# A planned order of all engines, searched anew after the first TensorE operations get a higher price

## The chip, the cores and the metric

The kernel runs on one core of a Trainium2 chip. The core has five engines that work beside each other and wait for each other through semaphores: TensorE (PE in the profile; PEld is its loading of weights), VectorE (DVE), ScalarE (ACT), GpSimd (POOL) and SyncE (SP), which here only issues DMAs. The metric is the device time of one execution in microseconds (us).

## The reference

Cosine attention over 8 batches, 12 heads, 448 positions and 64 channels is followed by a layer of two matrix products with a gate between them:

```
q_n = q / (norm(q) + 1e-6);  k_n = k / (norm(k) + 1e-6)
attn = softmax(q_n @ k_n.T / tau);  a = attn @ v
x = a with heads side by side                # 3584 x 768
h = x @ w_in                                 # 768 x 2048
out = (h * sigmoid(1.702 * h)) @ w_out       # 2048 x 768
```

## The kernel before

**Tiles.** A "group" y is four heads of one batch; a batch has three groups, so that there are 24, y = 0 to 23. Two heads of a group form a pair x = 2y or 2y + 1. For a group, k and q are loaded by SP (L263 for group 0, L271 for the others), squared (`square`, L304 on VectorE or GpSimd, L305 on ScalarE), summed by VectorE (`reduce`, L313), turned into an inverse norm (batch 0: roots on ScalarE, L325, and reciprocals on VectorE, L336; later batches: Newton steps on VectorE, `norm_a` and `norm_b`, L344 to L372), and scaled (`scale`, L404 for k, L405 for q). Groups 0 to 4 are transposed by TensorE (`turn_qk`, L427, 7 transposes for k and 7 for q) and copied out of PSUM (L438); later groups are transposed by DMAs that SP issues (L445). The last keys are copied apart (`last_keys`, L454). TensorE makes scores into a PSUM tile "sp" with two buffers (L465, last keys L491), ScalarE makes exponentials of them (L500), and TensorE multiplies these with v (`attend`, L528 and L539, 14 matmuls for a pair and half of the positions); v is cast by `cast_v` (L416 to L421). VectorE normalises (L551, L567); the result x is transposed by TensorE (L577 for batch 0, L586) and copied (L604, L593), or by a DMA (L610).

**Two halves in batch 0.** In batch 0 (`first`) the scores are made for the first half of the query positions of all three groups (h = 0) and then for the second (h = 1), so that the products can begin with half of batch 0.

**Products.** `mm1_h` (L651, batch 0) and `mm1` (L621) multiply x with w_in. A unit is 12 matmuls of half width or 6 of full width; ScalarE takes its tanh (L631), VectorE multiplies ("gate", L663 or L638, result gT). A unit holds one of the four buffers of the PSUM tile "mm" until its gate is done; attention, transposes and the second products take the same four. `mm2` (L676) multiplies gT with w_out in parts of four matmuls; parts 0 and 1 of a product need the first half of w_out, parts 2 and 3 the second. `halve` (L689 on VectorE, L690 on ScalarE) scales the result into one of two output tiles, and two stores on SP (L695) free it.

**DMA queues.** Loads, stores and DMA transposes are issued by SP in the planned order, one behind the other; w_in (L700, eight pieces) and w_out (L706, two pieces) by GpSimd. The loads of groups 4 and 5 are held until pieces of w_in have landed, w_out until the load of q of group 5 has landed, and those of group 6 until all of w_out has landed (`HOLD`).

**What sets the order.** `Plan` (L61 to L183) has an entry for every operation: engine, duration in us, due time, operations it comes after, buffers that it takes and frees. `Plan.tune` shifts the due time of each operation by one letter of `DUES` (a quarter of a us for a step) and chooses for those with an alternative engine one by a digit of `ENGINES`. `Plan.order` then plays the durations through at building time and lets every engine take the ready operation with the least due time. The kernel's instructions are emitted in that order, and every engine carries out its own in order. Durations in the plan thus take no part in the run itself; they and the two strings, which a search found, set only who comes first and on which engine.

Of the kernel before, what the change touches and what calls it, by code (L numbers as in the profile page):

```python
# [29 lines left out]
    "L]Zj_ZKtWtgIZL]]dHKIFKJRtM6KKOSAL;R7DKKNKAKKKL4IQL?KKMKKNAMKOKITMtMKS#EKKPONKHBhIhEbK;XZkNKKQNUK/KEPKKEt"  # L30
    "KJAH5KKKKKKNYKgR#tL4D]dN=BNGIQtJhOKLHCK=Egs%E/UFUKJDQ4NK:KKBKKE^bPPGJtKTBEA+4FK^KD41BRK^NLGE_SVLEKSKFKPt"
    "IRJMKWGtUILRKI;Y/KJKKKKRC8KKKKKJKFNM@FCKMTKNKYSKJ(tKGLAFK9JKJHKJM:KHiVSKRBKK:CHnKV@l^KJNgLKKKLSKmqolSsqT"
    "_if>NtslUJ=tKtaKt^PtiQE5$SKtKistHDEIgKKnjpK2cdjat;A[KiDVt<LMD#KNb=ISKLMKT]t]GKaKAKKt_XK<Kko9s^XNJtLrb:Kt"
    "LKht]L8ttKGstCZEtKKcLKcMCKDKKF%KKTOGVme3DV?aSQGKIN?OOKOEM(JHdL/DVtIpKAOKEK]>KKQGjKKVtIKfKB>/U?RLGIKLWKKK"
    "tXA^KLGNNKKtkHKJjJVgt#DStKKsKbhKFA%,KsOKtpKKirKHKhtKsJtBrt2,XLKKcIMLJZJLgK_JKKCJKNSe@3E8UNDYWKK#UX#S^Nti"
    "KL9K_CtE:RTKNHOBKStIt5K.L^:%tJSKBKKtKKJ0#LKKpOOKKLKHKlgKDKLKKKVKDKTKKL3Q#hK#J#KKKHebHjKPV#KK3EW9@<#t#9WB"
    "RWII#TI#BKKJOMHK0JMH@LNZjWKK2CO;HM#BEM8X8pKKK#P/O(8K-KK%YH#WGGKX]QIK51Br<:F7IHY-(KKOTQcKHBKKZZ_aka^SLKK#"
    "..KM:A4KKTjBMGM<LFEQ5KI#LK<IIEWK@KK?&KK#I#KKYKmK#^+##;&*K4EGKKJ+Q3KQKHGFJ#JMT#)KUC#IG>XKKI@JDJKGHIIHK)OT"
    "SNKJKtKQUKgCcKY$UKsFYAKGTAKRZKKDVHKN4*E0%DfKI9TQPKNKCJK@>>KKKK%:%^6MKKAPH<;KNKH5KKN1KIkFKt4FD#BFMKKK<#KK"
    "<N<M^PEXK#VE5KKKKAI.KG#KJKDKUEK:LJUB#K<<KO&&bHNC#NKKK&FK6@0<K#S/Q%LKAL6K3)D,1/)P%U#9?#MK#KM#QM<OPCMM#MPZ"  # L40
    "t;2G#FB4=7KP5@7FKK1KK#K:-9=KtPKd;K8BNL_@D$KK:LKQEL>KKKFF+<KQDsFK0@3fIGGKKbG?KnDBL;KF9KKAKkfLKHMSQKPO[IPL"
    "R%KK)BjCnK$KKKL#PNJ_GSsFPCXM-NNLEJtKFDHK>mK#KKKL=_ZKeSJKBtj@NQHDfF&VKKNZIdEKKK0ITKDSSF#MKOH3RRKJ;O6K(6R^"
    "t)DK#KKFKPBOOEBDKCIKoLBKML==PKqSIKOM9JIs?K;IL@(LKKK=KHIGM9YPBWKOBVVKGKKXfLDKKTFDDDte@?EH-EKC##[YFKKOGK0N"
    "Q#M?[YKTHEQUR.K+@H#HKKF?K%PIK>INKG_UHQ>JV:CNDRVKRJNMIJKLHOKFI5-JFKDKKKGHMEUT>M_QONKK@#KYJTRRSJS($MDKHKIM"
    "KKK:DCF;=YK(KKNWZK^KKK[RRHFU;HP=KK;KL9$@OKKMQHQFE3MGB#MKF?,OHBW^##V=V56KPPWUETaMKSKHMK*IKBKLNBE@K@GJSKI#"
    "FtKttL"
)
ENGINES = (
    "00021100010101000101000001100010000001010200000011012001110101102001100120001000010001020100120000000210"
    "10021111001001000201101100111100000101200111020100100210000201001011100012011010121101021111101100000011"  # L50
    "0011110110001011000010101110101011101010100010"
# [135 lines left out]
def kernel(  # L187
# [535 lines left out]

    def due_of(y):
        return 2 * y if y < ND else 4 * y
# [12 lines left out]
    for y in range(NDUO):  # L738
# [53 lines left out]
        if y < TURNED:  # L792
            for ti in (1, 0):
                add(("tp", ti, y), "PE", 0.45, s - 3, partial(turn_qk, y, ti),
                    after=[("scale", ti, y)] + [("tp", 1, y)] * (not ti and y > 1), takes=[("mm", 1), ("qkT", ti)], frees=[("qks", 2)])
                add(("qkT", ti, y), "DVE", 0.65, s - 3, partial(turned_qk, y, ti), after=[("tp", ti, y)], frees=[("mm", 1)], alts=[("ACT", 0.92)])
# [11 lines left out]
        if first:  # L808
            for h in range(2):
                sh = s + 2 * ND * h  # L810
                behind = [("s", min(y + 1, ND - 1), 2, 0)] * h
                for g in range(3):
                    add(("s", y, g, h), "PE", 0.23, sh + 0.4 * g, partial(scores_h, y, g, h), after=ready + behind + [("s", y, 0, h)] * (g > 0),
                        takes=[("sp", 1), ("exp", int(h + g == 0))], rows=64)
                    add(("exp", y, g, h), "ACT", 0.92, sh + 0.4 * g + 0.1, partial(exp_h, y, g, h), after=[("s", y, g, h)], frees=[("sp", 1)])
                add(("s", y, "l", h), "PE", 0.19, sh + 0.6, partial(scores_l, y, h), after=ready_l + behind + [("s", y, 0, h)],
# [181 lines left out]
```

## Time and profile before

| | us |
|---|---|
| median of 5 runs (lowest, highest) | 432.1 (430.6, 432.86) |
| profiled execution: time | 431.62 |
| profiled execution: span from first to last instruction | 429.8 |
| busy: TensorE | 408.1 (95%) |
| busy: VectorE | 292.8 (68%) |
| busy: ScalarE | 253.8 (59%) |
| busy: GpSimd | 122.2 (28%) |

A row of the profile's timeline has a start and a duration in us, the engine, the line of the kernel, the operation, "out<-in" and a count where like instructions are merged; in brackets stands the idle time before it and what ended it. "PEclk" and the clock of a stretch are the TensorE clock that was granted, of 10 or of 1. Matmuls overlap, so the step from one start to the next, not the duration of one, is what a matmul costs in a row of them.

### The profile page before, as it was taken

What the parts mean: (1) busy time and instruction counts of PE and PEld (TensorE: products, weight loads), DVE (VectorE), ACT (ScalarE), POOL (GpSimd) and SP (SyncE); (2) the same over time, 40 slices, a digit from 0 to 9 for tenths busy, and PEclk for the clock granted to TensorE, in tenths of its full rate; (3) what the DMA queues carried; (4) which work ended last, traced back from release to release, by engine and by line L of the source; (5) the groups of instructions that cost most, each with busy time, mean ns of one, the idle gap of its engine ahead of it and who ended that gap; (6) DMA issues with size and microseconds to landing.
All of it is one profiled execution on the core that took longest, in us unless ns stands there. A gap on an engine that the chain in (4) does not pass through costs nothing.

```text
span 429.8 us, 9183 instructions
## 1 busy us (share of the span) xinstructions
PE 408.1 (95%) x3600; PEld 242.6 (56%) x3600; DVE 292.8 (68%) x710; ACT 253.8 (59%) x374; POOL 122.2 (28%) x200
## 2 busy tenths in 40 slices
PE   1789999889999999999999999999999999999996
PEld 0567887454556554655556555565556655655563
DVE  4797996669899868997889778659757315424500
ACT  5689875846656677766861578756665455204310
POOL 5666532272520713042432052462000000000000
PEclk9969999999999999999999999999999999999999
DMA  8999899997879994979969956969535340221022
GB/s 273 234 207 259 153 210 223 290 204 182 191 151 218 186 231 113 197 150 210 217 117 235 169 163 121 200 170 138 82 45 85 78 96 0 23 73 38 0 75 73
DMA packets 86538, 65.34 MB, mean 152 GB/s; under 512 B 54624, under 2 KB 81504, under 8 KB 86496
## 3 DMA queue, kind: packets, MB, share of 16 engines
q1 hardware_dynamic: 82304, 57.82, 62.4%
q0 software_dynamic: 3744, 6.29, 8.3%
q10 hardware_dynamic: 448, 0.66, 0.4%
q8 instruction: 28, 0.46, 0.4%
q14 instruction: 14, 0.11, 0.1%
HBM read 47.19 MB, written 11.01 MB: 135 GB/s over the span
## 4 chain that ended last, share of the span: by engine, by line
PE 86%; DMA 7%; ACT 3%; DVE 3%; SPq 0%; POOL 0%; issue 0%; ACTq 0%; POOLq 0%; DVEq 0%
PE mm L676 32%; PE mm L621 28%; PE mm L539 8%; PE sp L465 8%; DMA qk<-in_k_dram 4%; PE mm L651 4%; PE mm L528 3%; DMA qk<-in_q_dram 3%; PE sp L491 2%; ACT exp L500 2%; PE mm L427 1%; DVE qks L404 1%; DVE gT L638 1%; ACT sq L305 0%; POOL sq L304 0%
## 5 line engine op out<-in xcount | busy, mean ns | idle before, releaser
L500 ACT ACTIVATE exp<-sp 128x896 f16<-128x896 f32 (+1 forms) x171 | 147.2, 903 | 61.9 <-PE sp L465 53.4
L676 PE MATMUL mm<-w_out,gT 128*128 128x384 f16 x896 | 156.8, 326 | 0.0
L621 PE MATMUL mm<-xT,w_in 128*128 128x448 f16 x672 | 134.4, 353 | 2.0 <-ACT ost L690 1.4
L676 PEld LDWEIGHTS <-gT 128*128 128x128 f16 x896 | 83.8, 98 | 62.1 <-issue 9.6
L631 ACT ACTIVATE th<-mm 128x448 f16<-128x448 f32 x128 | 69.8, 547 | 56.6 <-PE mm L621 50.3
L621 PEld LDWEIGHTS <-w_in 128*128 128x128 f16 x672 | 64.0, 98 | 64.2 <-issue 7.0
L638 DVE SCALAR_TENSOR_TENSOR gT<-th,mm 128x448 f16<-128x448 f16 x112 | 67.9, 617 | 41.1 <-ACT th L631 39.7
L313 DVE TENSOR_REDUCE n<-sq 128x14 f32<-128x896 f32 (+1 forms) x50 | 51.7, 1043 | 10.2 <-ACT sq L305 6.8
L539 PE MATMUL mm<-vt,exp 128*128 128x65 f16 (+1 forms) x1152 | 57.4, 197 | 0.0
L539 PEld LDWEIGHTS <-exp 128*128 128x128 f16 (+1 forms) x1152 | 53.1, 101 | 2.3
L528 PE MATMUL mm<-vt,exp 128*128 128x130 f16 x192 | 43.5, 226 | 1.8 <-DVE xs L567 1.8
L465 PE MATMUL sp<-qkT 64*128 64x448 f16 (+1 forms) x324 | 42.9, 346 | 1.5 <-ACT exp L500 1.3
L567 DVE TENSOR_TENSOR xs<-mm,rc 112x256 f16<-112x256 f32 x96 | 40.7, 424 | 3.5 <-PE mm L577 0.2
L304 POOL TENSOR_TENSOR sq<-qk 128x896 f32<-128x896 f32 (+1 forms) x17 | 29.0, 1703 | 33.4 <-DMA qk<-in_q_dram 13.4
L689 DVE TENSOR_SCALAR ost<-mm 128x384 f32<-128x384 f32 x27 | 14.8, 554 | 34.7 <-PE mm L676 34.6
L454 POOL COPY kL<-qkT 64x128 f16<-64x128 f16 x36 | 13.2, 368 | 81.3 <-DVE vt L421 37.2
L690 ACT ACTIVATE ost<-mm 128x384 f32<-128x384 f32 x29 | 14.1, 494 | 35.8 <-PE mm L676 33.6
L551 DVE RECIPROCAL rc<-mm 112x4 f32<-112x4 f32 x96 | 17.0, 177 | 24.7 <-PE mm L539 23.9
L305 ACT ACTIVATE sq<-qk 128x896 f32<-128x896 f32 (+1 forms) x27 | 24.4, 907 | 13.6 <-DMA qk<-in_k_dram 5.8
L404 POOL TENSOR_TENSOR qks<-qk,y 128x384 f16<-128x384 f32 (+1 forms) x27 | 18.7, 721 | 39.5 <-DVE y L372 17.4
L416 POOL CAST vt<-v 128x384 f16<-128x384 f32 x28 | 15.6, 556 | 43.6 <-PE mm L539 18.9
L528 PEld LDWEIGHTS <-exp 128*128 128x128 f16 x192 | 19.4, 101 | 13.4 <-issue 8.1
(59 smaller groups left out, 266.1 us busy)
## 6 DMA issues: line engine op xcount, KB each, us to landing
v<-in_v_dram SPq DMA_DIRECT2D x48, 256.0 KB, 5.7
out_dram<-ost SPq DMA_DIRECT2D x54, 192.0 KB, 3.3
qk<-in_k_dram SPq DMA_DIRECT2D x23, 448.0 KB, 5.0
qk<-in_q_dram SPq DMA_DIRECT2D x23, 448.0 KB, 5.1
w_in<-in_moe_w_in_dram POOLq DMA_DIRECT2D x8, 384.0 KB, 14.8
w_out<-in_moe_w_out_dram POOLq DMA_DIRECT2D x2, 1536.0 KB, 15.2
qkT<-qks SPq DMA_TRANSPOSE x38, 4.5
xT<-xs SPq DMA_TRANSPOSE x18, 3.9
```

Of the source, the lines that this page charges most:

```text
L304: return engines[eng].tensor_tensor(out=dst, in0=src, in1=src, op=ALU.mult)
L305: return nc.scalar.activation(out=dst, in_=src, func=AF.Square)
L313: return nc.vector.tensor_reduce(out=n2s[y][:, ti, js], in_=sqs[y, ti][:, js], axis=AX.X, op=ALU.add,)
L465: nc.tensor.matmul(out=sp[:, j, at : at + qn], lhsT=qkT[r, g, 1, 128 * n : 128 * (n + 1)], rhs=qkT[r, g, 0, q0 : q0 + qn], start=True, sto ...
L500: return nc.scalar.activation(out=dst, in_=src, func=AF.Exp, scale=inv_tau, **ekw)
L528: nc.tensor.matmul(out=o, lhsT=e[:, (C - 1) * S + a : (C - 1) * S + a + m], rhs=vt[:, 3].rearrange("p j d -> p (j d)"), start=True, stop=F ...
L539: nc.tensor.matmul(out=o[:, (D + 1) * j : (D + 1) * (j + 1)], lhsT=e[:, at : at + m], rhs=vt[:, n, j], start=False, stop=n == 2, skip_grou ...
L567: return nc.vector.tensor_tensor(out=xs, in0=ps[:, :, :D], in1=r[:, :, None].to_broadcast((P, 4, D)), op=ALU.mult,)
L621: nc.tensor.matmul(out=ps[:, :S], lhsT=w_in_sb[:, kk, 128 * m : 128 * (m + 1)], rhs=xTs[b, kk], start=(kk == 0), stop=(kk == KT1 - 1),)
L631: nc.scalar.activation(out=ths[key], in_=mms[key][:, :S], func=AF.Tanh, scale=0.851)
L638: nc.vector.scalar_tensor_tensor(out=gts[b // 2][:, m, (b % 2) * S : (b % 2 + 1) * S], in0=ths.pop((b, m)), scalar=1.0, in1=mms.pop((b, m) ...
L676: nc.tensor.matmul(out=mms[b2, t, n][:, :NW], lhsT=gts[b2][:, kk, 128 * t : 128 * (t + 1)], rhs=w_out_sb[:, kk, NW * n : NW * (n + 1)], st ...
```

## The change

TensorE's operations of groups 0 and 1 in the first half (h = 0) have about double their old durations in the plan: 7 transposes 0.78 for 0.45 (groups 0 and 1, and k of group 2), scores 0.38 for 0.23, scores of last keys 0.36 for 0.19, attention of a pair 0.95 for 0.5, transposes of x 0.24 for 0.15. With these, the search was made anew: most letters of `DUES` and many digits of `ENGINES` are others. Lines behind L722 move down by three; those named above keep their numbers.

```diff
--- before.py
+++ after.py
@@ -27,28 +27,28 @@
 MOE_FROM, MOE_LAG = 8, 9
 STEPS = "#$%&()*+,-./0123456789:;<=>?@ABCDEFGHIJKLMNOPQRSTUVWXYZ[]^_abcdefghijklmnopqrst"
 DUES = (
-    "L]Zj_ZKtWtgIZL]]dHKIFKJRtM6KKOSAL;R7DKKNKAKKKL4IQL?KKMKKNAMKOKITMtMKS#EKKPONKHBhIhEbK;XZkNKKQNUK/KEPKKEt"
...
+    "QOKKQJKNLtKK#brJGVRLHLVELKOHFKKKKdKKHCRAP>RJLKVDLMKX&SK<KEWUK_HHJCWAJKHsFK:lKtKiUeP9O5KLC;NaOJJMKF4CqQMN"
...
 )
 ENGINES = (
-    "00021100010101000101000001100010000001010200000011012001110101102001100120001000010001020100120000000210"
...
+    "00021100111111100110101001100011001011101211000000010001110111120000011112011010000001200100020110002211"
...
 )
 
 
@@ -720,6 +720,9 @@
     for y in range(2 * ND, NDUO, ND):
         groups += [(y,), (y + 1, y + 2)]
     group_of = {y: g for g in groups for y in g}
+
+    def cold(y, h):
+        return y < 2 and not h
 
     def due_of(y):
         return 2 * y if y < ND else 4 * y
@@ -791,7 +794,7 @@
                 takes=[("vt", 1)], frees=[("v", g)], alts=[("DVE", 0.86)])
         if y < TURNED:
             for ti in (1, 0):
-                add(("tp", ti, y), "PE", 0.45, s - 3, partial(turn_qk, y, ti),
+                add(("tp", ti, y), "PE", 0.78 if first and y < 2 + ti else 0.45, s - 3, partial(turn_qk, y, ti),
                     after=[("scale", ti, y)] + [("tp", 1, y)] * (not ti and y > 1), takes=[("mm", 1), ("qkT", ti)], frees=[("qks", 2)])
                 add(("qkT", ti, y), "DVE", 0.65, s - 3, partial(turned_qk, y, ti), after=[("tp", ti, y)], frees=[("mm", 1)], alts=[("ACT", 0.92)])
             add(("kL", y), "POOL", 0.63, s - 2, partial(last_keys, y), after=[("qkT", 1, y)] + kept(y),
@@ -810,10 +813,10 @@
                 sh = s + 2 * ND * h
                 behind = [("s", min(y + 1, ND - 1), 2, 0)] * h
                 for g in range(3):
-                    add(("s", y, g, h), "PE", 0.23, sh + 0.4 * g, partial(scores_h, y, g, h), after=ready + behind + [("s", y, 0, h)] * (g > 0),
+                    add(("s", y, g, h), "PE", 0.38 if cold(y, h) else 0.23, sh + 0.4 * g, partial(scores_h, y, g, h), after=ready + behind + [("s", y, 0, h)] * (g > 0),
                         takes=[("sp", 1), ("exp", int(h + g == 0))], rows=64)
                     add(("exp", y, g, h), "ACT", 0.92, sh + 0.4 * g + 0.1, partial(exp_h, y, g, h), after=[("s", y, g, h)], frees=[("sp", 1)])
-                add(("s", y, "l", h), "PE", 0.19, sh + 0.6, partial(scores_l, y, h), after=ready_l + behind + [("s", y, 0, h)],
+                add(("s", y, "l", h), "PE", 0.36 if cold(y, h) else 0.19, sh + 0.6, partial(scores_l, y, h), after=ready_l + behind + [("s", y, 0, h)],
                     takes=[("sp", 1)], frees=[("qkT", h), ("kL", h)])
                 add(("exp", y, "l", h), "ACT", 0.55, sh + 0.7, partial(exp_l, y, h), after=[("s", y, "l", h)], frees=[("sp", 1)])
         else:
@@ -836,7 +839,7 @@
                 else:
                     at = s + 2 * g + 2 + 0.5 * h
                     es = [("exp", y, g, n) for n in range(3)] + [("exp", y, "l")]
-                add(("at", x, h), "PE", 0.5, at, partial(attend, x, h, first and not h), after=es + [("cast", x)] + [("at", x, 0)] * h + [("at", x - 1, 1)] * (g * h),
+                add(("at", x, h), "PE", 0.95 if first and cold(y, h) else 0.5, at, partial(attend, x, h, first and not h), after=es + [("cast", x)] + [("at", x, 0)] * h + [("at", x - 1, 1)] * (g * h),
                     takes=[("mm", 1)], frees=[("exp", g * h), ("vt", h)])
                 turned = y < TX
                 whole = turned and not first
@@ -844,7 +847,7 @@
                     after=[("at", x, h)] + [("nx", 2 * y, 0)] * (not turned and g + h > 0) + [("nx", x, 0)] * (whole and h),
                     takes=[("xs", int(turned if first else h == 0 and (turned or g == 0)))], frees=[("mm", int(not turned or (whole and h == 0)))])
                 if turned and first:
-                    add(("turn", x, h), "PE", 0.15, at, partial(turn_h, x, h), after=[("nx", x, h)], frees=[("xs", 1)])
+                    add(("turn", x, h), "PE", 0.24 if cold(y, h) else 0.15, at, partial(turn_h, x, h), after=[("nx", x, h)], frees=[("xs", 1)])
                     add(("x", x, h), "DVE" if h else "ACT", 0.28 if h else 0.35, at, partial(turned_h, x, h), after=[("turn", x, h)] + [("x", 2 * y, 0)] * (g + h > 0),
                         takes=[("x", 2 * (g + h == 0))], frees=[("mm", 1)],
                         alts=[("ACT", 0.35) if h else ("DVE", 0.28)])
```

The order in which each engine's instructions stand is fixed when the program is built, and so can be read for the new kernel too. What differs, in numbers:

| operation | before | after |
|---|---|---|
| squares of a whole q or k on ScalarE, GpSimd, VectorE | 24, 16, 6 | 21, 19, 6 |
| k scalings on VectorE, GpSimd | 14, 10 | 11, 13 |
| q scalings on VectorE, GpSimd | 12, 12 | 10, 14 |
| copies of transposed q or k on VectorE, ScalarE | 7, 3 | 5, 5 |
| casts of v (pairs) on VectorE, GpSimd | 20, 28 | 17, 31 |
| last-key copies on VectorE, GpSimd | 12, 36 | 24, 24 |
| half copies of x on VectorE, ScalarE | 10, 2 | 5, 7 |
| whole copies of x on VectorE, ScalarE | 2, 4 | 1, 5 |
| halvings on VectorE, ScalarE | 27, 29 | 23, 33 |
| TensorE before the first product with w_in: transposes of q and k, half scores, full scores, attention matmuls, x transposes | 56, 68, 4, 154, 20 | 56, 72, 0, 140, 18 |
| TensorE before the first part that needs the second half of w_out: half scores, full scores, attention matmuls, x transposes, mm2 | 68, 28, 280, 36, 8 | 72, 24, 238, 28, 8 |
| TensorE before the third unit of batch 1: half scores, full scores, mm2 | 68, 40, 92 | 72, 36, 96 |

In the order after, GpSimd scales q of group 1 before it issues w_in, and q of group 2 behind it; VectorE sums the squares of q of group 4 before the first gate (before: behind the second); ScalarE has the square of q of group 9 ahead of the first tanh of batch 1 (before: behind the second); SP has the loads of group 8 ahead of the first store, and the DMA transposes of group 6 ahead of the second.

## The prediction

> **What bounds the kernel now.** I read the page first (busy shares, the forty slices, the chain that ended last), then the stretches of two microseconds in the first 34, then TensorE's instructions in order of time, and last the landings and waits of the DMAs that TensorE needs.
>
> ```profile
> span 429.8 us, 9183 instructions
> PE 408.1 (95%) x3600; PEld 242.6 (56%) x3600; DVE 292.8 (68%) x710; ACT 253.8 (59%) x374; POOL 122.2 (28%) x200
> ...
> PEclk9969999999999999999999999999999999999999
> ...
> PE 86%; DMA 7%; ACT 3%; DVE 3%; SPq 0%; POOL 0%; issue 0%; ACTq 0%; POOLq 0%; DVEq 0%
> ```
>
> TensorE is busy 408.1 of 429.8 us and holds 86% of the chain: there are 21.7 us without a matmul. Its 3600 matmuls are the same after the change, so the time is TensorE's work plus its idle time plus the excess at a low clock. By TensorE's timeline the idle time is 7.97 before the first matmul, about 5 up to 30, 0.28 at 43, 1.84 at 84, 1.36 at 93, 0.68 at 104 and 4.1 behind the last matmul (0.49 for the last halving and the store). From 104.4 to 425.7 no gap shows.
>
> ```profile
> core 0: us, PE busy (x) PEld busy (x) DVE busy (x) ACT busy (x) POOL busy (x), PEclk, DMA share, GB/s
> 24.00:26.00 2.00, 1.97 (x15) 1.27 (x15) 1.95 (x5) 1.82 (x3) 1.79 (x5) 0.56 1.12 239
> 26.00:28.00 2.00, 1.56 (x16) 0.88 (x16) 1.96 (x5) 1.97 (x4) 1.60 (x3) 0.50 1.14 219
> 28.00:30.00 2.00, 2.00 (x26) 1.58 (x25) 1.46 (x6) 1.40 (x2) 0.92 (x3) 0.50 1.12 210
> 30.00:32.00 2.00, 2.00 (x32) 1.66 (x30) 1.73 (x8) 1.12 (x4) 0.00 (x0) 0.73 1.12 209
> ...
> 16.33 0.93 PE L427 MATMUL mm<-ident,qks 128*128 128x128 f16 x7
> ...
> 39.54 2.46 PE L651 MATMUL mm<-xT,w_in 128*128 128x224 f16 x24
> 43.48 2.46 PE L651 MATMUL mm<-xT,w_in 128*128 128x224 f16 x24 [0.28 <-DVE gT L663]
> ...
> 50.37 0.55 PE L427 MATMUL mm<-ident,qks 128*128 128x128 f16 x7
> ```
>
> In the stretches the tenth number, after five pairs of busy time and count, is the granted clock: 0.50 to 0.73 from 24 to 32. The seven transposes at 16.33 took 0.93 together, the same seven at 50.37 took 0.55, although the clock row has 1.00 at 16: matmuls ran slowly there too. So the old price of one transposing group (0.45) was too low early. The first product with w_in starts at 39.54.
>
> ```profile
> 67.64 1.46 PE L676 MATMUL mm<-w_out,gT 128*128 128x384 f16 x8
> ...
> 70.15 2.11 PE L676 MATMUL mm<-w_out,gT 128*128 128x384 f16 x12
> ...
> 85.91 0.23 PE L528 MATMUL mm<-vt,exp 128*128 128x130 f16 x1 [1.84 <-DVE xs L567]
> ...
> 94.36 2.43 PE L621 MATMUL mm<-xT,w_in 128*128 128x448 f16 x12 [1.36 <-ACT ost L690]
> ...
> 104.38 1.29 PE L621 MATMUL mm<-xT,w_in 128*128 128x448 f16 x6 [0.68 <-DVE gT L638]
> ```
>
> The products with w_out start at 67.64; the part that needs the second half of w_out is in the twelve at 70.15 (about 70.3, behind the last part of x = 8). Then come three stalls, 1.84 + 1.36 + 0.68 = 3.9.
>
> ```profile
> L706 POOL DMA_DIRECT2D w_out<-in_moe_w_out_dram x2: 893/920/946, 50.0 to 50.9; - x2
> DMA to landing us min/median/max: 11.6/15.2/18.8
> ...
> SPq L271 <- DMA w_in<-in_moe_w_in_dram: 18.0, 2, 10.5
> SPq L271 <- DMA w_out<-in_moe_w_out_dram: 3.0, 1, 3.0
> ```
>
> w_out is issued in two pieces at 50.0 and 50.9; they land 11.6 and 18.8 later, at 61.6 and 69.7. Loads behind them on SP wait for w_in and w_out pieces, 18.0 and 3.0 us. DMAs were busy more than 1.0 in nearly every stretch from 10 to 48 and again from 54 to 70. These landings are a clock that TensorE's order cannot hurry.
>
> **The change part by part.** (1) Only the planner's prices and the two search strings change. No matmul comes or goes: 0 us of work. Scores and transposes of groups 0 and 1 are spread differently on TensorE.
>
> (2) Other engines, by the rows' means and the new counts. VectorE loses three k scalings (2 x 0.813 + 0.304 each), two q scalings (1.1), three casts (0.55 + 0.23 + 0.27), two transposed copies (0.62), one whole and five half x copies (0.39, 0.27) and four halvings (0.55), and gains twelve last-key copies (0.21): about -13.7 us. ScalarE gains two transposed copies (0.91), five half and one whole x copy (0.36, 0.53), four halvings (0.49) and loses three squares (0.95): +3.3. GpSimd gains three squares (1.75), three k and two q scalings (2.2, 1.74), three casts (1.15) and loses twelve last-key copies (0.37): +14.3. They are busy 68%, 59% and 28%, TensorE's work lies over them: 0 on the path in total. If this cover went, the price is where one of them stands in front of a matmul, below.
>
> (3) Up to the first product. The new order copies both transposed halves of group 0 on ScalarE and squares group 2 before the first exponential: that starts near 15.4 instead of 14.88 (qkT of q at 13.85 + 0.91, then 0.56 of scores). GpSimd scales q of group 1 (1.69) before it issues w_in, so w_in starts near 18.7 instead of 17.34; behind its eight issues (5.2) comes the scaling of q of group 2, done at 25.5, where VectorE had it at 24.1. ScalarE's list from there to the last x copy is 12.6 us (eight or nine exponentials of 0.82 back to back, short ones of 0.46, copies) on top of about 23.3: 35.9 without gaps; with the 13% idle that it had in 20 to 40 about 38. Ends: 35.9 and, with the slow clock as long as now, 40.5. I take 38.5: a gain of 1, less 0.9 of work not yet done.
>
> (4) The gain is not kept. VectorE's new order puts the sum of squares of q of group 4 ahead of the first gate; before, two gates went first (42.8). That load landed at 41.5:
>
> ```profile
> 41.54 1.68 POOL L304 TENSOR_TENSOR sq<-qk 128x896 f32<-128x896 f32 x1 [3.44 <-DMA qk<-in_q_dram]
> ```
>
> So the first gate ends at 41.54 + 1.68 + 1.07 + 0.61 + 0.1 = 45.0, and the fourth product unit, which takes its PSUM buffer, starts then. Queued behind it on TensorE are attention and the other units. Counted by the steps from one matmul to the next at full pace in the rows (12 half-width products 1.15, 14 attention matmuls 0.50, 4 full scores 0.48), TensorE has done 20.7 us of work at 45.0; before, it had done 21.9 (25.0 at 48.08). Price at that point: 1.2, plus what the load slips.
>
> (5) w_out. Its issue waits for the load of q of group 5 and, on GpSimd, for k of group 4 to be scaled: 45.0 + 0.9 (Newton) + 0.6 (gate) + 0.3 + 1.3 + 2.0 = 50.1, against 49.96. Landings 61.7 and 69.8. Slip of w_in: between 0 (DMAs saturated, same bytes) and 1.3 (the later start); I take 1.0, nearest to the later start, because loads 4 and 5 wait for w_in pieces. At the part that needs the second half, the new order has done 42 attention matmuls (0.036 each), 8 x transposes (0.06) and 4 full scores (0.12) less and 4 half scores (0.075) more than the old: 1.5 + 0.5 + 0.5 - 0.3 = 2.2. It stands at 69.8 where the old was at 70.3 with 2.2 more done: +1.8 (rounded up for the switch between row modes), with the slip +2.8.
>
> (6) From 74 to 105. The old stalls of 3.9 belong to waits that are reordered (-3.9 if all go). New ones: on ScalarE the squares of k and q of group 7 stand before an exponential; k landed at 82.4, so that it ends near 85.9 and TensorE's next scores wait 1.2. The square of q of group 9 stands before the first tanh of batch 1; before, it stood behind two of them:
>
> ```profile
> 95.08 0.95 ACT L305 ACTIVATE sq<-qk 128x896 f32<-128x896 f32 x1 [0.33 <-DMA qk<-in_q_dram]
> ```
>
> Its load was issued at 86.46 and waited for until 95.08. Issued at 85.1 (the load whose completion it waits for, v of group 7, was issued at 73.3 and took 11.8) it lands between 93.6 and 95.0, then 0.95 + 0.54 + 0.61 until the third unit of batch 1 gets its buffer: 95.8 to 97.2, some 1.0 behind TensorE. The second store of the first output tile is queued behind the two transposes of group 6 on SP (5.4); the third tile's halving waits for that store, and VectorE's gates behind it: 0 to 3, I take 0.8. Sum of new stalls 3.0.
>
> (7) Behind 105 VectorE has at most 16 us of work in 16 us of TensorE's: bounded by 0 and 3, taken 0 as the old trace shows no gap there. The end is the same 128 products, halving and store: 0.
>
> Sum: +1.8 + 1.0 - 3.9 + 3.0 = +1.9 on the profiled 431.62 (span 429.8 and 1.8 around it): 433.5. The median of the five runs is 432.1, 0.5 higher: **434.0**.
>
> A rule against the change stands in the Trainium skill, TensorE: Matmul & The Clock Gate, section Part 1: The HAM clock gate: the slow phase is a time of about 3.4 us in a free-running window, not a set of matmuls, differs between runs, costs under 1% and should not be fitted. By that (an estimate) all that could be won is under 4.3 us, and a price tied to named operations can miss. This trace agrees in part: the slow stretch came back from 24 to 31, and cost about 2.9.
>
> **The rivals.** Each decides against the median of 432.1; 0.3% (1.3 us) is about what a measurement tells from no change.
> - A, forecast: the landings hold TensorE, new stalls replace old. 434.0, own range 432.6 to 436.
> - B, faster: the three stalls from 84 to 104 vanish and nothing replaces them, as exponentials and gates get a VectorE with 13.7 us less to do. For it: two of the three ended with VectorE or an output halving. Against: the loads that ScalarE now meets first. +1.8 + 0 to 1.0 - 3.9 = -2.1 to -1.1: 430.0 to 431.0. It decides once new stalls and slip together stay under 2.1.
> - C, no change: slip 0 and new stalls of 2.1, or the order moves work under the same landings only: 432.1.
> - D, much slower: the store behind the transposes holds VectorE for its full 3, the slip is 1.3 and one stall of 3 comes behind 105: 1.8 + 1.3 - 3.9 + 5.2 + 3 = +7.4, near 439.5; with half of it 436.
>
> **How the numbers follow.** A 0.47 (0.10 of it within 0.3%), B 0.25, C 0.13, D 0.15. Faster 0.25, same 0.23, slower 0.52. Range 429.4 to 439: the lower end takes in B with 0.6 of run scatter, the upper D nearly whole; under 0.15 is outside.
>
> **What would show it.** In the new profile: first product near 38.5; an idle of 1 to 3 before a product with w_in near 44, ended by VectorE's gate; the products with w_out waiting for its DMA near 70; the third unit of batch 1 near 96 with a wait on a gate; no gap behind 105. I am wrong if w_out lands before 68, if TensorE stands ahead of 47 us of work at 70.3, or if gaps come late.

## The result, and the profile after

The new kernel takes 432.66 us (median; 430.07 to 436.02), the old one beside it 431.01 us. The ratio on record is 1.0055, with a 95% interval from 1.0042 to 1.0069: slower by half a per cent, where the forecast was 434.0 on 432.1, a ratio of 1.0044. Ratios, here and below, are given as they were recorded, and are not quotients of the medians beside them; these two medians divide to 1.0038, a difference of 1.65 us.

The profiled execution of the new kernel took 434.07 us with a span of 432.0. From its page:

```profile
span 432.0 us, 9195 instructions
PE 407.6 (94%) x3600; PEld 242.6 (56%) x3600; DVE 278.9 (65%) x690; ACT 256.1 (59%) x383; POOL 135.9 (31%) x211
...
PEclk9989999999999999999999999999999999999999
...
PE 75%; DMA 12%; DVE 8%; POOL 3%; issue 1%; ACT 1%; SPq 0%; POOLq 0%; DVEq 0%; ACTq 0%
```

TensorE's work is the same (407.6 for 408.1), so the span grew by idle time: 24.4 us without a matmul for 21.7. VectorE has 13.9 us less to do, GpSimd 13.7 more, ScalarE 2.3 more. TensorE's share of the chain that ended last fell from 86% to 75%; DMA and VectorE took it.

The granted clock in stretches of 2 us (the tenth number of a row):

```profile
24.00:26.00 2.00, 1.50 (x14) 1.03 (x15) 1.48 (x4) 1.98 (x4) 1.88 (x4) 0.85 1.19 202
26.00:28.00 2.00, 2.00 (x24) 1.38 (x21) 1.48 (x6) 1.50 (x3) 0.78 (x3) 0.50 1.11 206
28.00:30.00 2.00, 2.00 (x36) 1.31 (x34) 1.78 (x9) 1.51 (x3) 0.00 (x0) 0.80 1.15 211
30.00:32.00 2.00, 1.94 (x34) 1.59 (x33) 1.66 (x6) 1.84 (x3) 1.67 (x2) 1.00 1.13 213
```

By these rows the slow stretch from 24 on is about half as long as in the old profile. The rows before 24 read 1.00 in both profiles, although matmuls still ran slowly there: seven transposes at 20.48 took 0.93 in the new one. TensorE's timeline, idle time in brackets:

```profile
36.51 0.56 PE L427 MATMUL mm<-ident,qks 128*128 128x128 f16 x7 [1.00 <-POOL qks L405]
...
39.40 2.46 PE L651 MATMUL mm<-xT,w_in 128*128 128x224 f16 x24
...
43.22 1.31 PE L651 MATMUL mm<-xT,w_in 128*128 128x224 f16 x12 [0.77 <-ACT xT L604]
...
45.16 1.31 PE L651 MATMUL mm<-xT,w_in 128*128 128x224 f16 x12
...
70.87 0.81 PE L676 MATMUL mm<-w_out,gT 128*128 128x384 f16 x4
...
90.10 0.36 PE L586 MATMUL mm<-ident,xs 112*128 112x112 f16 x4 [0.27 <-DVE xs L567]
...
95.20 2.43 PE L621 MATMUL mm<-xT,w_in 128*128 128x448 f16 x12 [0.51 <-DVE gT L638]
...
126.84 0.23 PE L528 MATMUL mm<-vt,exp 128*128 128x130 f16 x1 [0.70 <-DVE xs L567]
...
161.57 0.22 PE L528 MATMUL mm<-vt,exp 128*128 128x130 f16 x1 [1.40 <-DVE gT L638]
...
260.73 0.22 PE L528 MATMUL mm<-vt,exp 128*128 128x130 f16 x1 [0.18 <-DVE gT L638]
```

The old stalls of 3.88 between 84 and 105 have become 0.78. Three gaps stand behind 105, where the old trace shows none: 0.70 + 1.40 + 0.18 = 2.28. Read backwards, a span less its idle time behind 105 (without the tail, 4.2 in both) says how late TensorE is at 105: 429.8 - 0 in the old profile, 432.0 - 2.28 = 429.7 in the new. By this reckoning the kernels are level at 105 in these two profiles, and the whole difference comes behind it. Two executions, with spans that scatter from 428.0 to 433.9 over the new kernel's 44 runs, are a thin ground for that; the experiments had to show it.

The two largest late gaps have one form. VectorE's own rows ahead of them:

```profile
123.42 2.81 DVE L404 TENSOR_TENSOR qks<-qk,y 128x384 f16<-128x384 f32 x3
126.15 0.17 DVE L551 RECIPROCAL rc<-mm 112x4 f32<-112x4 f32 x1
...
158.93 1.09 DVE L313 TENSOR_REDUCE n<-sq 128x14 f32<-128x896 f32 x1 [2.03 <-ACT sq L305]
...
160.91 1.68 DVE L638 SCALAR_TENSOR_TENSOR gT<-th,mm 128x448 f16<-128x448 f16 x3
```

At 123.42 the scaling of k of group 11 stands in front of the normalising that TensorE needs. At 158.93 the sum of squares of q of group 14 stands in front of three gates and itself waits 2.03 for a square on ScalarE, whose load had only just landed. Neither result is needed soon.

### The profile page after: what moved, and what is told of

Read it like the earlier page. It is cut to its first block, busy times and chain, and to the rows that moved or that the text cites. A ratio compares the mean times of both kernels' runs of the same rounds, so it can differ in the third digit from the quotient of the medians.

```text
span 432.0 us, 9195 instructions
## 1 busy us (share of the span) xinstructions
PE 407.6 (94%) x3600; PEld 242.6 (56%) x3600; DVE 278.9 (65%) x690; ACT 256.1 (59%) x383; POOL 135.9 (31%) x211
## 4 chain that ended last, share of the span: by engine, by line
PE 75%; DMA 12%; DVE 8%; POOL 3%; issue 1%; ACT 1%; SPq 0%; POOLq 0%; DVEq 0%; ACTq 0%
PE mm L676 31%; PE mm L621 25%; DMA qk<-in_q_dram 7%; PE mm L539 7%; PE sp L465 6%; PE mm L651 2%; PE mm L528 2%; DMA w_in<-in_moe_w_in_dram 2%; DMA v<-in_v_dram 2%; PE sp L491 1%; DVE n L313 1%; DVE qks L404 1%; POOL sq L304 1%; DVE gT L638 1%; DVE gT L663 1%
## 5 line engine op out<-in xcount | busy, mean ns | idle before, releaser
L621 PE MATMUL mm<-xT,w_in 128*128 128x448 f16 x672 | 135.8, 353 | 0.5 <-DVE gT L638 0.5
L539 PE MATMUL mm<-vt,exp 128*128 128x65 f16 (+1 forms) x1152 | 56.0, 195 | 0.0
L539 PEld LDWEIGHTS <-exp 128*128 128x128 f16 (+1 forms) x1152 | 52.0, 100 | 4.8 <-issue 1.9
L304 POOL TENSOR_TENSOR sq<-qk 128x896 f32<-128x896 f32 (+1 forms) x20 | 33.7, 1685 | 40.5 <-DVE sq L304 13.4
L690 ACT ACTIVATE ost<-mm 128x384 f32<-128x384 f32 x33 | 16.2, 491 | 36.8 <-PE mm L676 29.0
L689 DVE TENSOR_SCALAR ost<-mm 128x384 f32<-128x384 f32 x23 | 12.7, 556 | 34.7 <-PE mm L676 34.6
L404 POOL TENSOR_TENSOR qks<-qk,y 128x384 f16<-128x384 f32 (+1 forms) x36 | 23.8, 689 | 31.4 <-issue 15.0
L305 ACT ACTIVATE sq<-qk 128x896 f32<-128x896 f32 (+1 forms) x24 | 21.6, 902 | 8.7 <-DMA qk<-in_q_dram 5.3
L454 POOL COPY kL<-qkT 64x128 f16<-64x128 f16 x24 | 7.9, 329 | 48.2 <-DVE y L361 20.8
```

The source lines that it names most:

```text
L304: return engines[eng].tensor_tensor(out=dst, in0=src, in1=src, op=ALU.mult)
L404: return tuple(eng.tensor_tensor(out=o, in0=a, in1=b, op=ALU.mult) for o, a, b in places(y))
L539: nc.tensor.matmul(out=o[:, (D + 1) * j : (D + 1) * (j + 1)], lhsT=e[:, at : at + m], rhs=vt[:, n, j], start=False, stop=n == 2, skip_grou ...
L621: nc.tensor.matmul(out=ps[:, :S], lhsT=w_in_sb[:, kk, 128 * m : 128 * (m + 1)], rhs=xTs[b, kk], start=(kk == 0), stop=(kk == KT1 - 1),)
```

## The experiments

All reorderings use one edit: the planned order is taken as a list, and a few named operations are put right behind a later one (`anchor`). Every engine's work stays the same unless said.

```diff
-        for _, i, emit in self.order():
+        order = list(self.order())
+        at = {names[i]: (now, i, emit) for now, i, emit in order}
+        for anchor, late in MOVES:
+            late = [at[n] for n in late]
+            order = [o for o in order if o not in late]
+            k = order.index(at[anchor]) + 1
+            order[k:k] = late
+        for _, i, emit in order:
```

Each time is a median of 6 to 12 runs beside 17 to 35 runs of the old kernel on the same chip; ratios are to the old kernel. Line numbers in the rows below are shifted by the lines that each edit inserts (by 2 to 13, and by 62 where the order is written out as lists).

### One half of the change at a time

**The new strings with the old prices.** The five conditional prices go back to 0.45, 0.23, 0.19, 0.5 and 0.15.

> The new search strings (due times and engines) under the old prices; the order is another again. Theory: the strings fit one planner only, so the order away from the prices it was found with is worse than both: new stalls where one engine's instruction stands in front of another that TensorE needs, ratio to before 1.01 to 1.04. Rival: the prices of a few early operations do not matter behind 40 us and the strings carry the result: ratio 1.003 to 1.008, like the new kernel.

**The old strings with the new prices**, all but that of the q and k transposes, which stays 0.45 (below, the line of the new kernel and that of this run).

```diff
-                add(("tp", ti, y), "PE", 0.78 if first and y < 2 + ti else 0.45, s - 3, partial(turn_qk, y, ti),
+                add(("tp", ti, y), "PE", 0.45, s - 3, partial(turn_qk, y, ti),
```

> The old search strings under the new prices of scores, attention and x transposes of the first two groups (the new price of the q and k transposes left out). Theory: as above, an order away from its search is worse, ratio to before 1.01 to 1.04; the prices by themselves are no gain. Rival: the truer prices are what helps early, and the strings only repair the rest: ratio under 1.003, with the first product with w_in before 39.4.

Measured: 450.34 us, 1.0452 (1.0413 to 1.0491), and 446.38 us, 1.0380 (1.0324 to 1.0437). One gap from TensorE's timeline of each, strings first:

```profile
57.11 0.22 PE L528 MATMUL mm<-vt,exp 128*128 128x130 f16 x1 [2.64 <-DVE gT L663]
```

```profile
147.59 0.56 PE L465 MATMUL sp<-qkT 64*128 64x448 f16 x2 [2.82 <-ACT exp L500]
```

The second lies more than 110 us behind the last operation whose price was changed. Strings and prices belong together here: the prices of 21 early operations can shift every later choice of the planner, and both sets of strings are 4% worse with prices that they were not found with. What the change does to the time is therefore the new order as a whole, and no part of it can be called the effect of the prices.

### Does the early half pace cost anything?

Sixteen matmuls whose result nobody reads are added to the old kernel, where TensorE is idle:

```diff
+    def warm(n):
+        sp = ps_s.tile([128, 2, 512], FP32, name="sp")
+        for i in range(n):
+            nc.tensor.matmul(out=sp[:, i % 2], lhsT=ident, rhs=kLs_all[:, :2].rearrange("p a b c -> p (a b c)"), start=True, stop=True)
+
+    warm(12)    # and warm(4) behind the first seven transposes
     plan.tune(DUES, ENGINES)
```

> The old kernel, with sixteen extra matmuls of a 128 x 128 by a 128 x 512 operand whose result nobody reads: twelve in TensorE's first idle 8 us, four behind the first seven transposes. Only work is added; what the change's new prices are about (matmuls at half pace up to 22 us) should go. Theory: the first 40 us are set by loads, VectorE, ScalarE and GpSimd, not by TensorE's pace; the seven transposes near 16 take 0.55 instead of 0.93, and the first product with w_in comes less than 0.5 earlier than 39.5; ratio to before 0.998 to 1.002. Rival (the half pace is on the path, and a plan that counts it is worth having): the half-pace excess up to 22, about 4 (the rows from 8 to 22 add up to 8.9 us busy, at full pace about 5), and the slow stretch of 2.9 come off; ratio 0.985 to 0.993.

The clock did the opposite of what both theories took for granted. Stretches of 8 us, then 2 us:

```profile
8.00:16.00 8.00, 6.07 (x35) 3.00 (x35) 7.33 (x14) 6.04 (x11) 5.18 (x11) 0.51 1.11 274
16.00:24.00 8.00, 7.38 (x70) 4.79 (x66) 5.69 (x15) 5.68 (x9) 7.35 (x17) 0.50 1.15 253
24.00:32.00 8.00, 7.54 (x76) 5.45 (x73) 6.71 (x21) 5.95 (x8) 3.83 (x9) 0.50 1.11 216
32.00:34.00 2.00, 2.00 (x40) 1.41 (x38) 0.87 (x4) 1.64 (x3) 1.10 (x2) 0.97 1.09 262
...
40.23 2.46 PE L653 MATMUL mm<-xT,w_in 128*128 128x224 f16 x24
```

The granted clock was 0.50 from 8 to 32 us; the seven transposes that were to take 0.55 took 0.93 as before. So this run tests the reverse: in the old profile the pace was full from 20.9 to 24 and again from 31 on (by its transposes, scores and clock rows), here it is half throughout, about 4 us more. The first product with w_in comes at 40.23 instead of 39.54; but in three later profiles with the same early order and no added matmuls it comes at 39.21, 39.92 and 40.52, so no cost can be read from that. The stalls of 84 to 105 are 1.84 + 1.60 + 0.73 where they were 1.84 + 1.36 + 0.68, and the kernel takes 432.7 us: 1.0014 (0.9987 to 1.0041), although its median lies 1.7 above the 431.02 of the runs beside it. About 4 us more at half pace cost nothing that these runs can tell from no change. Full pace throughout was not reached in the old order, so what it would win stays open.

The Trainium skill (TensorE: Matmul & The Clock Gate, Part 1: The HAM clock gate) says that about 3.4 us of sustained work bring the full clock. Here TensorE was busy 7.38 of 8 us from 16 to 24 at 0.50, so this row disagrees. That its window runs free of the kernel, so that the switch falls elsewhere each time, fits these profiles: with the same early order, scores took 0.37 at 21.57 in the old profile (full pace), but still 0.56 at 21.13 and at 28.76 in that of a run further below (old first half, new rest), which has no added matmuls. The clock row alone can't tell this: in the next run's profile it reads 1.00 throughout, though seven transposes took 0.93 at 20.93 and at 26.14.

### The early stalls

**Three stalls mended.** The sum of squares of q of group 4 goes behind the first gate, a cast behind the scaling of q of group 3, and one x copy from ScalarE to VectorE.

```diff
+ MOVES = ((('g', 0, 0, 'h'), [('red', 0, 4)]), (('scale', 0, 3), [('cast', 6)]))
+            eng = {('x', 2, 1): 'DVE'}.get(names[i], eng)
```

> The new kernel, with three of its early stalls mended by order alone: the sum of squares of q of group 4 goes behind the first gate instead of ahead of it (stalls at 45.16 and, behind it, 48.50), a cast of v goes behind the scaling of q of group 3 on GpSimd (1.00 at 36.51), and one x copy goes from ScalarE, where it stands behind the table load, to VectorE (0.77 at 43.22). Theory: the lag of 2.9 that TensorE has at 70.9 against the old kernel is the sum of these engine stalls; TensorE reaches the part with the second half of w_out 1.5 to 2.5 sooner and the time falls by as much, ratio to before 0.9995 to 1.002. Rival (the prediction's step 5: the landing of w_out near 70.3 holds TensorE however fast it comes): a wait for w_out of 1 to 2 shows at 70, the time falls by less than 0.6, ratio 1.004 to 1.0055.

Measured: 432.59 us, 1.0052 (1.0022 to 1.0082): nothing won. The rival named the right outcome, but not the right place:

```profile
42.00 1.32 PE L662 MATMUL mm<-xT,w_in 128*128 128x224 f16 x12
43.64 1.31 PE L662 MATMUL mm<-xT,w_in 128*128 128x224 f16 x12
46.47 0.22 PE L539 MATMUL mm<-vt,exp 128*128 128x130 f16 x1 [1.52 <-DVE gT L674]
...
70.88 0.81 PE L687 MATMUL mm<-w_out,gT 128*128 128x384 f16 x4
```

The fourth unit starts at 43.64 instead of 45.16; then TensorE waits 1.52 for the second gate, which now stands behind the sum of squares. At 70.88 it is where the new kernel was (70.87). The load of q of group 4 holds VectorE's list, whichever gate is behind it.

**w_out first.** GpSimd issues w_out ahead of its scaling of k of group 4.

```diff
+ MOVES = ((('g', 0, 2, 'h'), [('w_out', 0), ('w_out', 1)]),)
```

> The new kernel, with GpSimd's two issues of w_out ahead of its scaling of k of group 4 instead of behind it; they still wait for the load of q of group 5. Theory: TensorE is late at 70.9 by the stalls from 36 to 54, not by w_out (the landing at 70.3 shows no wait): w_out lands 1 to 2 sooner and nothing follows; the scaling comes up to 2 later and may cost up to 1; ratio 1.004 to 1.008. Rival (the prediction's step 5, the slip of w_out costs what it slips): the time falls by 1 to 2; ratio 1.000 to 1.003.

Measured: 432.19 us, 1.0037 (1.0011 to 1.0062). The interval reaches into both ranges; no decision. Nor did the edit move what it was meant to move: the issues came at 49.9 and 50.9 (50.0 and 50.9 before), with GpSimd idle for 4.60 ahead of them, and the second piece landed at 69.4 instead of 70.3. The scaling came later, and TensorE waited 0.76 for it at 54.36.

**Both, and the whole chain behind that load out of the gates' way.**

```diff
+ MOVES = ((('g', 0, 4, 'h'), [('red', 0, 4), ('norm', 0, (4,))]),
+          (('g', 0, 6, 'h'), [('norm', 1, (4,)), ('scale', 1, 4)]),
+          (('scale', 0, 3), [('cast', 6)]),
+          (('g', 0, 2, 'h'), [('w_out', 0), ('w_out', 1)]))
+            eng = {('x', 2, 1): 'DVE'}.get(names[i], eng)
```

> The new kernel, with the chain behind the load of q of group 4 (its sum of squares, both halves of the norm, the scaling of k) behind three and four gates instead of ahead of the first, the cast and the x copy of the run with early stalls mended, and w_out issued ahead of that scaling. In the runs so far TensorE came to the fourth unit 0.4 to 0.7 sooner or later and always waited until that load's chain was through (45.16, 45.85, 46.47). Theory: that chain in front of the gates is what costs the new order its 2.9 at 70; the fourth unit starts before 44.5, TensorE stands 1 to 2 better at 70, ratio 1.000 to 1.003. Rival (w_out's second half or the later scaling of group 4 take it back): no stall at 45 but one of 1 to 2 between 52 and 71, ratio 1.004 to 1.008.

Measured: 431.95 us, 1.0028 (1.0000 to 1.0056). In its profile w_out is issued at 46.7, the fourth unit starts at 41.80 and the part with w_out's second half at 69.00, but 1.41 goes back at 51.09, where TensorE waits for the scaling that was put off. By the point values about half of the loss is undone by an early lead of almost 2 us; the interval reaches from all of it to none. Each theory named one part: no stall at 45, and one of 1.4 behind it.

### Which half of the order loses?

The planned order and the engines are written into the kernel as lists: the first 319 of 1670 steps (to about 70 us) from one kernel, the rest from the other. The two sets of 319 differ by four steps, so the seam is clean.

```diff
-    plan.tune(DUES, ENGINES)
+    plan.choose(ENGINES)      # an engine for each step, from the kernel that the step is taken from
...
-        for _, i, emit in self.order():
+        for i in ORDER:           # 319 steps of the one kernel's order, 1351 of the other's
+            emit = self.ops[names[i]][3]
```

> The old kernel's order and engines for its first 319 planned steps (all up to about 70 us, through the last part of w_out's first product), the new kernel's for the other 1351; the two sets of first steps differ by four steps only. In the profiles so far, TensorE's idle time behind 60 and ahead of the tail was 3.9 and 4.2 in the old order and 3.1, 1.8, 1.2, 1.1 and 1.1 in kernels with the new order, and span less this idle time was 425.9 and 426.6 against 428.0 to 430.2 less such mends. Theory: the new order loses about 2.9 up to 60 and wins about 2.1 behind 70; this run keeps only the gain: ratio 0.993 to 0.998, faster than both. Rival (step 7 of the prediction is what failed, the late stalls at 126 and 161 are the loss and the early part is even): ratio 1.003 to 1.007.

> The reverse: the new order and engines for the first 319 steps, the old for the rest. Theory: only the early loss is left, and the old stalls from 84 to 104: ratio 1.006 to 1.012, slower than both. Rival: ratio 0.998 to 1.002.

| first 319 steps | the rest | median, us | ratio to the old kernel |
|---|---|---|---|
| old | new | 432.58 | 1.0053 (1.0028 to 1.0077) |
| new | old | 431.03 | 1.0018 (0.9990 to 1.0046) |
| new | new | 432.66 | 1.0055 (1.0042 to 1.0069) |

My theory falls: neither interval reaches into its ranges. Both values lie in the rival's ranges, so the loss seems to go with the order behind 70 us. That is supported and not proven, as the two intervals overlap between 1.0028 and 1.0046. The gaps of the first (late part new), then of the second (late part old) from 70 to the end:

```profile
83.57 0.36 PE L527 MATMUL sp<-qkT 64*128 64x448 f16 x2 [0.71 <-ACT exp L562]
...
89.88 0.36 PE L648 MATMUL mm<-ident,xs 112*128 112x112 f16 x4 [1.38 <-DVE xs L629]
...
126.17 0.23 PE L590 MATMUL mm<-vt,exp 128*128 128x130 f16 x1 [0.70 <-DVE xs L629]
...
258.47 0.22 PE L590 MATMUL mm<-vt,exp 128*128 128x130 f16 x1 [0.18 <-DVE gT L700]
```

```profile
73.27 0.36 PE L648 MATMUL mm<-ident,xs 112*128 112x112 f16 x4 [0.28 <-DVE xs L629]
```

The gaps of the first add up to 2.97, less than the 3.88 of the old kernel, and the spans of the two profiles are 429.7 and 429.8. So the profile does not show where the half that loses 0.53% loses it.

The second is the instructive one. The old order's stalls of 3.88 from 84 to 105 are gone without a single one of its operations being moved there. For the first of them the rows show how. TensorE in the old profile, then in this one (the same operations; the wait of 1.84 stands ahead of the row at 85.91):

```profile
82.60 1.46 PE L676 MATMUL mm<-w_out,gT 128*128 128x384 f16 x8
...
85.91 0.23 PE L528 MATMUL mm<-vt,exp 128*128 128x130 f16 x1 [1.84 <-DVE xs L567]
```

```profile
85.27 1.46 PE L738 MATMUL mm<-w_out,gT 128*128 128x384 f16 x8
86.56 0.22 PE L590 MATMUL mm<-vt,exp 128*128 128x130 f16 x1
```

TensorE comes 2.7 later out of the new early part, but the normalising that it waits for comes only 0.3 later (85.72 for 85.42), and the wait is gone. The second stall went in another way: ScalarE's halving that waited for a store until 93.82 runs at 92.35 without such a wait. So the early loss costs less in the end (0.18%, -0.10 to 0.46) than the 2.8 us or 0.65% that TensorE was behind at 70 in the new kernel's profile; how much less is open. The gaps near 126 and 260, in contrast, come back in both the new kernel and this half of it.

### The late stalls

**First mend.** Behind three gates, and behind a normalising:

```diff
+ MOVES = ((('g', 2, 4), [('sq', 0, 14), ('red', 0, 14), ('norm', 0, (13, 14))]),
+          (('nx', 15, 0), [('scale', 1, 11)]))
```

> The new kernel, with its two largest late stalls on TensorE mended by order alone: the square, the sum of squares and the first half of the norm of q of group 14 go behind the three gates that TensorE waited for at 161.57 (1.40), and the scaling of k of group 11 on VectorE goes behind the first normalising of x = 15, which TensorE waited for at 126.84 (0.70). No work comes or goes. Theory: behind 105 TensorE is the bound and every such stall is paid in full, so the time falls by 2.1, to about before plus 0.2 (ratio to before 1.0005, from 1.0055), with no gap at 126 and 161. Rival (the prediction's step 7, nothing behind 105 costs anything because other work or landings set the end): the time stays, ratio 1.005 to 1.006, and the gaps come back elsewhere.

Measured: 433.86 us, 1.0071 (1.0042 to 1.0100): no gain. The gap at 126 is gone, but the put-off work now stands in front of two normalisings and a gate:

```profile
163.26 1.31 PE L631 MATMUL mm<-xT,w_in 128*128 128x448 f16 x6 [1.06 <-DVE xs L577]
...
165.94 0.22 PE L538 MATMUL mm<-vt,exp 128*128 128x130 f16 x1 [0.28 <-DVE gT L648]
```

Moreover, in the four other profiles with the new late order untouched (early stalls mended, w_out first, both, and old early part) there is no gap near 161 at all: ScalarE waited 0 to 0.37 for the load ahead of that square, against 1.89 in the new kernel's profile. The gap depends on when that load lands. Those near 126 (0.69 or 0.70) and 260 (0.17 or 0.18) are in all four.

**Second mend.** The same operations further back, and the one near 260:

```diff
+ MOVES = ((('nx', 15, 0), [('scale', 1, 11)]),
+          (('g', 2, 8), [('sq', 0, 14), ('red', 0, 14), ('norm', 0, (13, 14))]),
+          (('g', 4, 4), [('scale', 1, 19)]))
```

> The new kernel, with its late stalls mended once more: the scaling of k of group 11 behind the first normalising of x = 15 (0.70 near 126, in all six profiles with the new late order but the one where it was mended), the scaling of k of group 19 behind one gate (0.18 near 260, in all of them), and the square, sum of squares and first norm half of q of group 14 behind five gates and two normalisings instead of three gates (1.40 at 161 in the new kernel, 1.34 at 163 to 166 in the first mend). The halves exchanged between the kernels have shown that the loss goes with the order behind 70. Theory: these stalls are that loss; 0.9 to 2.3 comes off, ratio 1.000 to 1.0035, no idle time over 0.4 from 100 to 420. Rival (the loss behind 70 is not in these stalls; they are waits for loads that only change place, or the time is lost outside what one profile shows): ratio 1.0045 to 1.007.

Measured: 431.74 us, 1.0032 (1.0005 to 1.0059). The value lies in the theory's range, and the interval reaches into the rival's. One gap is left, larger than the 0.4 expected:

```profile
164.34 0.81 PE L687 MATMUL mm<-w_out,gT 128*128 128x384 f16 x4 [0.66 <-DVE gT L649]
```

By the point values about 1 us of the loss goes (1.0055 to 1.0032), but the intervals of the two kernels overlap, and the idle time does not account for it: 0.66 is left behind 105 here, against 0.87 or 0.88 in the four profiles with the untouched late order and no gap near 161. The last of the early mends won as much (1.0028). So this fits the cause and does not prove it.

### The old kernel's own stalls

**All three mended**, by order alone:

```diff
+ MOVES = ((('nx', 10, 1), [('norm', 1, (6,)), ('red', 1, 7), ('scale', 1, 6)]),
+          (('g', 1, 5), [('scale', 1, 7)]),
+          (('st', 0, 0, 0, 1, 3), [('st', 1, 0, 0, 1, 3)]))
```

> The old kernel, its three stalls from 84 to 104 mended by order alone: the second half of the norm of group 6, the sum of squares of k of group 7 and the scaling that follows go behind two normalisings of x = 10 (stall 1.84 at 85.91); the second store of the first output tile goes right behind the first on SP's queue, ahead of the loads of v (1.36 at 94.36); the scaling of k of group 7 on VectorE goes behind three gates (0.68 at 104.38). Theory: from 75 on TensorE is the bound, and each of these is paid: up to 3.9 comes off, 2 to 3.9 as something else is later; ratio 0.991 to 0.996, and this beats both kernels. Rival (waits move on, because loads land when they land): ratio 0.997 to 1.003, with as much idle time in new places from 84 to 180.

Measured: 429.92 us, 0.9974 (0.9949 to 1.0000), in the rival's range. Of the three stalls 0.35 is left, at 87.89, and a new one came:

```profile
94.95 1.30 PE L632 MATMUL mm<-xT,w_in 128*128 128x448 f16 x6 [1.34 <-DVE gT L649]
```

**And that one mended too:**

```diff
+          (('g', 1, 0), [('red', 0, 8)]), (('g', 1, 2), [('red', 1, 9)])
```

> The old kernel with its three stalls mended as before, and the one that took their place: the sums of squares of q of group 8 and k of group 9 on VectorE go behind the first and behind the third gate of batch 1, where TensorE waited 1.34 at 94.95 for a gate that stood behind them. Theory: behind 75 TensorE is the bound, so another 1.0 to 1.3 comes off; ratio 0.993 to 0.996. Rival (what is late is the squares on GpSimd and the loads, and the wait moves on): ratio 0.996 to 0.999, with a new stall over 1 between 95 and 125.

Measured: 430.49 us, 0.9991 (0.9962 to 1.0019). The gap of 1.34 is gone, with 0.39 at 99.89 and 0.58 at 107.18 in its place; by the profile 0.4 less idle time, by the clock nothing. Idle time from 84 to 108 fell from 3.88 to 1.33, and the time by 0.4 to 1.1: the rival was nearer, though its stall over 1 did not come. The first of the two may beat both kernels by a quarter of a per cent; the second, almost the same, does not confirm it. Idle time in a profile is thus not paid one for one: 2.2 us less of it came with 1.1 us in the first of these kernels, 2.6 us less with 0.4 in the second.

## Why the prediction was right, and where its working was wrong

The direction and the size were right: slower, +1.9 forecast on one profile's time, a ratio of 1.0044 against 1.0055. The sum came to that by two errors of opposite sign, 2.2 too much in step (6) and 2.3 too little in step (7); that they cancelled was luck.

- **Steps (1) and (2)** hold: VectorE -13.9 (forecast -13.7), GpSimd +13.7 (+14.3), ScalarE +2.3 (+3.3), TensorE's work the same.
- **Step (3)**: the first product at 39.40, not 38.5, inside the range of 35.9 to 40.5. The gain taken for it did not come; TensorE lost 1.00 to the scaling of q of group 3, which the new order gave to GpSimd behind three casts.
- **Step (4)** is right about the gate, to a tenth, but not about TensorE's wait for it. The gate behind the sum of squares of q of group 4, forecast to end at 45.0, ended at 45.1, and the fourth unit started at 45.16 (VectorE's and GpSimd's rows, then TensorE's ahead of that unit):

```profile
41.78 1.68 POOL L304 TENSOR_TENSOR sq<-qk 128x896 f32<-128x896 f32 x1 [2.20 <-DMA qk<-in_q_dram]
...
43.50 1.09 DVE L313 TENSOR_REDUCE n<-sq 128x14 f32<-128x896 f32 x1 [2.75 <-POOL sq L304]
44.50 0.61 DVE L663 SCALAR_TENSOR_TENSOR gT<-th,mm 128x448 f16<-128x448 f16 x1
...
44.48 0.54 PE L491 MATMUL sp<-qkT,kL 128*128 128x448 f16 x2
```

  TensorE was at work until 45.02 and stood 0.14 for the gate. It was late already, by the 1.00 at 36.51 and by the 0.77 at 43.22, which a copy of x on ScalarE ended; the sign that was forecast, an idle time of 1 to 3 near 44 ended by VectorE's gate, is not there. In other profiles with the same early order TensorE waits for that gate 1.54 (first late mend) or 0.79 (old late half), and not at all in the second late mend:

```profile
45.85 1.31 PE L661 MATMUL mm<-xT,w_in 128*128 128x224 f16 x12 [1.54 <-DVE gT L673]
```

```profile
44.78 1.31 PE L713 MATMUL mm<-xT,w_in 128*128 128x224 f16 x12 [0.79 <-DVE gT L725]
```

- **Step (5)** gave TensorE a lag of 2.8 at the part with w_out's second half. It was about that: 2.2 us of work less done by the counted operations, and the part started 0.6 later (70.87 against 70.31). But its cause was half wrong. The issue slipped by nothing (50.0), the second piece landed at 50.9 + 19.4 = 70.3, and TensorE came 0.6 later without a wait: the lag was made by the stalls from 36 to 54 (1.00 + 0.77 + 0.14 + 0.41 + 0.41 = 2.7), not by the landing. The 0.1 added for a switch between row modes is shown by no run.

```profile
L706 POOL DMA_DIRECT2D w_out<-in_moe_w_out_dram x2: 893/920/946, 50.0 to 50.9; - x2
...
DMA to landing us min/median/max: 11.9/15.7/19.4
```

- **Step (6)**: the old stalls went (-3.9 forecast, -3.88 in the profile). The new ones, taken as 3.0, were 0.78: the scores' wait of 1.2 and the store's 0.8 did not come, and the unit forecast for 95.8 to 97.2 started at 95.20 with a wait of 0.51. With (4) and (5) this makes the kernels about level at 105. The prediction would have had them 1.9 apart there.
- **Step (7)**, "taken 0 as the old trace shows no gap there", is the term that was furthest off. It measured 2.28 in the profile, within its own bound of 0 to 3, and late gaps were one of the prediction's own signs of being wrong. The exchange of halves points the same way: with the old order behind 70 the loss is 0.18% (-0.10 to 0.46), with the new one 0.53% (0.28 to 0.77). An old trace without gaps says that the old order has none; a new order of nearly the same busy shares can have them. That these gaps are the loss is not shown, for the half with the new late order has less idle time than the old kernel.
- **Its base**: the sum took 1.8 around the span as given. It is 1.80 in the old kernel's runs and 2.08 in the new one's (medians), so 0.3 of the loss lies outside the span. It goes more with the early half (1.98 with the new early part and the old rest, 1.84 the other way round); what it is, no view here shows.
- **The rivals**: B (the stalls from 84 to 104 vanish and little replaces them) happened in the profile, without making the kernel faster: the lag of 2.8 at 70, at the top of what B allowed, and the 2.28 behind 105, which it left out, took it back. D's stall behind 105 came in three smaller ones, its store did not.
- **The rule weighed against the change**: the end of the half pace differed between profiles of the same early order, and about 4 us more of it cost nothing measurable. What the new prices describe is real (transposes 0.93 for 0.55); that it is on the path, no run shows.

Still open is what makes the loss. Of 1.65 us between the medians 0.3 lies outside the span. The two gaps that recur behind 105 (0.88) and the one near 161 (1.40 in one profile of five) could be most of the rest, if idle time were paid in full; the mended old kernels and the half with the new late order show that it is not always. Single profiles can't decide it.

## What to carry to other kernels

Time won or lost on one engine can be given back at its next wait for another engine or a transfer: before pricing an early gain, look for those waits and ask whether they shrink or grow by as much. In engines that work in order, price a new order by what stands directly in front of each gate and normalising that the bound engine needs, through the whole kernel and not only where the change was aimed. To find which part of a reordering counts, exchange halves of the order between the kernels and time them, with more runs than the twelve here, whose intervals still overlap; a profile of each misleads when runs scatter by more than the effect.

## What was not expected of the hardware

Matmuls added in the first idle 8 us did not bring the full clock forward: twelve of them took 4.43 us from 1.39 on, and the granted clock was then 0.50 until 32, though TensorE was busy 6.07, 7.38 and 7.54 of 8 us in the three stretches. Against the old profile, where the pace was full for about 4 of these 24 us, the whole kernel was no more than 0.41% longer by the upper end of its interval.
